# A planner's release latencies, its settings and 32-row pieces of a down-projection in a fused attention and MLP kernel

## The chip, the cores and the metric

The kernel runs on one core of one Trainium2 chip. A core has five engines with a queue each: TensorE (PE in the profile; its weight loads are shown as PEld), VectorE (DVE), ScalarE (ACT), GpSimd (POOL) and SyncE (SP, which here only issues DMAs). The metric is the device time of one execution in microseconds, the median of several runs. The kernel before takes 757.61 us (three runs, 757.32 to 758.09).

## The reference

Two branches work on the same `x` of 2048 tokens by 512 values, and a sigmoid gate per token mixes them:

```python
q, k, v = split(x @ wqkv)                 # 32 heads of 16 values
a = softmax(q @ k.T / 4) @ v @ wo         # attention over 2048 keys
h  = gelu(layernorm(x) @ w1)
x1 = x + shift_tokens(h) @ w2             # 4 groups of channels shifted by 1, -1, 2, -2 tokens
b  = x1 + gelu(layernorm(x1) @ w3) @ w4   # 512 -> 1792 -> 512
out = g * a + (1 - g) * b                 # g = sigmoid(sum(x * gate_w))
```

With 32 heads and 2048 x 2048 scores per head, the exponentials are the largest job: 134 million of them.

## The kernel before

**Attention tiles.** The queries are cut into 4 chunks of 512. A score tile is 128 keys by 512 queries of one head, and there are 32 x 16 x 4 = 2048 of them (`TOT`, line 933). They are grouped in 32 rounds: chunk, group of 8 heads, and one of two halves of the group, so that a round has 4 heads, each in a row tile of TensorE of its own, with 16 key tiles per head (line 1219). A score matmul (`qk_op`, line 1254) contracts over 32 rows, so up to four of them run at once in the four row tiles. The product with V (`take_pv`, lines 1465 to 1489) contracts over 128 keys and fills 17 of 32 columns, so four of those run at once in four column tiles; they add up in one bank of PSUM, the accumulator of the round.

**Two ways to an exponential.** Either ACT takes two or three score tiles, 1024 or 1536 columns, in one instruction straight from PSUM (`issue_act`, line 1352); how many is decided by `CAP2` and `CAP3`, the number of banks that ACT's tiles may hold together. Or DVE turns a tile into the bits of an approximation (line 1383), and for each two such tiles three shifted copies are made, by DVE (line 1426) or by POOL (line 1428). An ACT tile needs one product with V, a DVE tile four. `GP2` and `GP3` set how the three copies are shared out: normally DVE makes the first two and POOL the third; for a share `GP2` of the pairs POOL makes two; for a share `1 - GP3` DVE makes all three (`close_pair`, line 1403).

**The other matmuls.** The projections and the MLP are cut into groups of 512 output columns (`gen`, line 911). A group is a list of units, one per block of 128 in the contraction, and each unit is four matmuls into four column tiles of the group's bank. The down-projection `w4` (`mlp2_down`, line 1166) has 14 units over the 1792 inner values, and, but for the last chunk, four more with `wo` over the packed attention output `oD`. DVE empties the bank of a group.

**End of a round.** The accumulator is copied out (line 1501); a chain of small DMAs (lines 1503 to 1516) brings the denominators to a reciprocal and spreads them over the partitions (`bcs`), POOL multiplies (line 1518), and four DMAs pack the result into `oD` (line 1522), from which the `wo` units read.

**What sets the order.** The order of all instructions is worked out when the program is built, by a small event-driven model of the engines (`Sim`, line 154). Each piece of work is a `Job` with a hold (how long its engine is taken) and a latency (how long after that its results and buffers count as there). PE's next visit is picked by `pe_pick` (line 1651): first score tiles for ACT, then tiles for DVE; when there is no room for those, up to `MAXU` passes of products with V and group units. `pe_run` (line 335) gives each its time: 216 ns for a pass of 512 columns, a switch between row tiles, column tiles and the full array (`SWITCH`, line 155), and a release 275 ns after the end (`PE_LAT`, line 157). Some forty settings (`BASE`, line 445) steer it, and `STEPS` (line 470) changes them at given places: step n takes effect at score tile 8n. On the chip only the order on each queue remains; semaphores make an instruction wait for its data and for its buffers.

Of the kernel before, what the change touches and what calls it, by code (L numbers as in the profile page):

```python
# [98 lines left out]
class Job:  # L99
    __slots__ = ("eng", "hold", "lat", "deps", "prio", "fn", "acq", "frees", "at", "done", "start", "seq", "ready", "name", "port", "watch", "deps_tiles", "size")  # L100

    def __init__(self, eng, hold, lat, deps, fn, prio=5, acq=(), frees=(), at=0, name="", port=False):
        self.port = port
        self.eng, self.hold, self.lat, self.deps, self.fn = eng, hold, lat, list(deps), fn
        self.prio, self.acq, self.frees, self.at = prio, list(acq), list(frees), at
        self.done = self.start = None
        self.seq = 0
        self.ready = None
        self.name = name
        self.watch = []  # L110
        self.size = 0


class Op:
    __slots__ = ("mode", "tile", "fn", "done", "start", "ns", "frees", "name", "watch", "dst")

    def __init__(self, mode, tl, fn, ns=216.0, frees=(), name=""):
# [7 lines left out]
class Gen:  # L125


    def __init__(self, units, deps, at, name, acq="bank", due=None):
# [6 lines left out]
        self.skew = False  # L135

    def left(self):
        return any(self.cp[j] < len(self.units) for j in range(4)) if self.skew else self.pos < len(self.units)

    def take(self, j):  # L140
        k = self.cp[j]
        if k == len(self.units):
            return None
        self.cp[j] = k + 1
        o = self.units[k][j]
        if min(self.cp) == k + 1:
# [5 lines left out]


class Sim:
    SWITCH = {"row": 122.0, "col": 96.0, "full": 96.0}
    ISSUE = 4.0
    PE_LAT = 275.0

    def __init__(self, slots):
# [23 lines left out]
        self.readers = {}  # L183

# [12 lines left out]
    def place(self, job):  # L197

        for d in job.deps:
            if d.done is None:  # L200
                d.watch.append(job)
                return
        self.jobs[job.eng].append(job)
# [84 lines left out]
    def try_engine(self, e):  # L288
# [22 lines left out]
        for b in j.acq:  # L311
            self.take(b)
        j.start = self.t
# [11 lines left out]
        self.push(self.t + j.hold, None)  # L325
        self.pending -= 1
# [8 lines left out]
    def pe_run(self, ops):  # L335
        cur = self.t
        for o in ops:
# [5 lines left out]
            else:  # L343
                s = max(self.arr[o.tile], cur + self.ISSUE)
            if o.tile is None:
# [7 lines left out]
            self.push(s + o.ns + self.PE_LAT, lambda o=o: self.finish_op(o))  # L353
# [39 lines left out]
def kernel(  # L393
# [73 lines left out]
        ROT=2, DUE_SH=-14, AT_SH=0, HOLE=7, MAXG=1, CAP2=6, CAP3=0, LIMD=3, RES=0, GATE=2, E_PRIO=2, AFIRST=0, AGE=12000, ACC2=0, LIMA=3, JOIN=0,  # L467
# [3 lines left out]
        0: dict(DVE_STOP=13, SL1=200, B_LOW=2, DVE_WAIT=1, PV_IDLE=0.5, PRESS=26, DUE_SH=0, AT_SH=34, CAP3=5, GATE=4,  # L471
            E_PRIO=0.25),
        1: dict(GP2=0.8),
        2: dict(GP2=0.655),
        3: dict(PV_FULL=0.97, LIMA=2),
        5: dict(DVE_STOP=8, SL1=60),
        6: dict(P1_PRIO=0.279),
        7: dict(GP3=0.8, B_LOW=1),
        8: dict(S_PRIO=0.178, GP3=0.967, B_LOW=2, AFIRST=1),
        9: dict(P1_PRIO=0.312, GP2=0.8, SL1=200, PV_FULL=0.916, PV_IDLE=0.731, ROT=0, HOLE=2, AFIRST=0, LIMA=3),  # L480
        10: dict(S_PRIO=0.38),
        13: dict(AT_SH=118),
        14: dict(ROT=2, AT_SH=96),
        16: dict(AHEAD2=9, PV_IDLE=0.5),
        19: dict(GP3=0.8, JOIN=1),
        20: dict(DVE_WAIT=2, AT_SH=0),
        21: dict(AFIRST=2),
        22: dict(URG=8),
        23: dict(GP3=0.9, DVE_STOP=6, DVE_ALONE=-81, DVE_WAIT=1, AHEAD2=13, PV_FULL=0.947, MAXU=3, ROT=1, AT_SH=34,
            HOLE=0, JOIN=0),  # L490
        24: dict(GP2=1),
        25: dict(DVE_STOP=13),
        26: dict(DVE_STOP=8, MAXU=5),
        29: dict(SL0=0),
        30: dict(SL0=45),
        31: dict(AHEAD=5),
        33: dict(DVE_STOP=6),
        34: dict(PRESS=18, MAXU=3),
        35: dict(P1_PRIO=0.414, GP3=1, URG=5, DVE_ALONE=138, AHEAD=9, PV_FULL=0.813, PV_IDLE=0.731, PRESS=26, E_PRIO=0.1,
            AGE=6000, JOIN=1),  # L500
        37: dict(ROT=3),
        39: dict(P1_PRIO=0.136, DVE_ALONE=500, DVE_WAIT=4),
        40: dict(MAXU=7, HOLE=2),
        41: dict(URG=11, AT_SH=96),
        42: dict(DVE_STOP=8, IDLE_NS=374, DVE_WAIT=2),
        44: dict(P1_PRIO=0.312),
        45: dict(P1_PRIO=0.136),
        46: dict(AT_SH=69),
        47: dict(S_PRIO=0.178, AGE=3000, LIMA=2),
        48: dict(ROT=1),  # L510
        51: dict(URG=2),
        52: dict(DVE_WAIT=1),
        53: dict(AGE=20000),
        54: dict(PV_FULL=0.97),
        55: dict(DVE_ALONE=2, PV_FULL=0.916),
        56: dict(AT_SH=118),
        59: dict(MAXU=4, ROT=0),
        61: dict(DVE_ALONE=138),
        62: dict(AGE=1000000000),
        63: dict(AGE=20000),  # L520
        65: dict(URG=11, ACC2=1),
        69: dict(AHEAD2=16, MAXG=2, AGE=1000000000),
        70: dict(AHEAD2=13, MAXG=1, AGE=20000),
        71: dict(PV_FULL=0.813, ACC2=0, LIMA=4),
        72: dict(S_PRIO=0.214, ROT=3),
        73: dict(S_PRIO=0.178, AHEAD2=16, PV_FULL=0.916, ROT=0, MAXG=2, AGE=1000000000, ACC2=1, LIMA=2),
        74: dict(AFIRST=1),
        76: dict(PV_IDLE=0.117, AGE=20000),
        77: dict(HOLE=7),
        79: dict(ROT=1),  # L530
        80: dict(ROT=2),
        81: dict(B_LOW=1, MAXU=3),
        82: dict(GP3=0.633, ROT=0, MAXG=1),
        83: dict(GP2=0.5),
        84: dict(GP3=0.8, LIMA=4),
        85: dict(P1_PRIO=0.279, URG=5, DVE_ALONE=2, SL1=0, IDLE_NS=864, B_LOW=8, DVE_WAIT=2, PV_FULL=0.813, PRESS=57,
            MAXU=2, ROT=2, DUE_SH=-9, HOLE=0, CAP2=4, CAP3=0, GATE=3, E_PRIO=2, AFIRST=0, LIMA=2, JOIN=0),
        86: dict(PV_FULL=0.916, ROT=1),
        87: dict(HOLE=7, ACC2=0),
        88: dict(GP3=0.9, PV_FULL=0.86, E_PRIO=0.1),  # L540
        89: dict(PRESS=26, AGE=1000000000),
        90: dict(B_LOW=2),
        91: dict(GP2=1, GP3=0.8, EARLY=64, B_LOW=8, PV_FULL=0.916, PRESS=57, E_PRIO=2, AGE=20000),
        92: dict(GP2=0.5, EARLY=99),
        93: dict(URG=8, DVE_ALONE=-81, AHEAD=24, PV_FULL=0.813, CAP2=5, AGE=1000000000, ACC2=1),
        95: dict(DVE_ALONE=2, LIMD=4, E_PRIO=0.4),
        96: dict(DVE_ALONE=-81, LIMD=3, E_PRIO=2),
        97: dict(S_PRIO=0.214, GP2=0, GP3=0.967, URG=5, DVE_ALONE=2, B_LOW=5, DVE_WAIT=4, AHEAD=9, PV_IDLE=0.731,
            PRESS=18, ROT=2, HOLE=3, CAP2=4, E_PRIO=0.4, ACC2=0, LIMA=3),
# [1346 lines left out]
```

## Time and profile before

| | |
|---|---|
| median of the runs | 757.61 us |
| profiled execution: time, span | 757.9 us, 756.0 us |
| busy PE, ACT, DVE, POOL | 740.8, 738.0, 674.2, 423.0 us |
| exponentials on ACT: 1024 columns, 1536 columns | 560, 133 instructions |
| score tiles on DVE (line 1383) | 529 |
| copies on DVE, on POOL | 436, 359 |
| score matmuls, products with V | 2048, 3635 |

The share of busy time must be read with care. An instruction's span in the trace reaches from its start to the end of its write, and the next one on the same engine starts before that, so an engine is shown busy even where it could have done more. The rate of an engine is read from the distance between starts, or from a merged row of many like instructions. For TensorE the chain of work (in which every visit to row tiles and every visit to column tiles is one piece, with the time until the next) says more than the busy time.

### The profile page before, as it was taken

The numbers are of one execution on the slowest core, as the hardware profiler recorded it, in microseconds if no ns is written. First come the engines' busy times: TensorE is split into PE (matmuls) and PEld (weight loads), VectorE is DVE, ScalarE is ACT, GpSimd is POOL, SyncE is SP. The second block draws the span as 40 slices with busy tenths as digits, with TensorE's granted clock in tenths as the row PEclk, the third lists the DMA queues.
The fourth block names the chain that finished last, engine by engine and source line by source line (L and its number), as shares of the span: only waits on it lengthen the run. The fifth ranks groups of instructions, "written<-read, shape, count | busy, mean of one in ns | idle before, by whom it ended". The sixth has DMA issues, their size and how long they took to land.

```text
span 756.0 us, 23489 instructions
## 1 busy us (share of the span) xinstructions
PE 740.8 (98%) x9464; PEld 213.2 (28%) x9464; DVE 674.2 (89%) x1399; ACT 738.0 (98%) x714; POOL 423.0 (56%) x421
## 2 busy tenths in 40 slices
PE   8999999999999999999999899999999999999997
PEld 4334222222222222223222222222222322222222
DVE  5899988889999999999999796798888989999886
ACT  6999999999999999999999899999999999999995
POOL 2265467776665465554554653477776855553431
PEclk9999999999999999999999999999999999999999
DMA  9423331012412200132001100100200000000001
GB/s 201 139 72 75 71 65 26 21 45 66 114 34 73 79 17 21 27 100 79 10 24 35 30 25 27 35 6 20 49 17 20 21 13 26 25 28 21 20 20 33
DMA packets 67093, 34.59 MB, mean 46 GB/s; under 512 B 46748, under 2 KB 62380, under 8 KB 66984
## 3 DMA queue, kind: packets, MB, share of 16 engines
q1 hardware_dynamic: 66040, 32.56, 17.0%
q8 instruction: 74, 1.21, 0.7%
q10 hardware_dynamic: 944, 0.52, 0.2%
q14 instruction: 35, 0.29, 0.1%
HBM read 17.40 MB, written 6.81 MB: 32 GB/s over the span
## 4 chain that ended last, share of the span: by engine, by line
PE 81%; ACT 11%; DVE 4%; issue 2%; DMA 0%; POOL 0%; ACTq 0%; DVEq 0%; POOLq 0%
PE banks L1257 28%; PE banks L1481 28%; PE banks L918 23%; ACT prob L1352 10%; DVE prob L1383 1%; DVE prob L1426 1%; ACT hB L1162 1%; PE banks L897 0%; PE banks L1817 0%; DMA oD<-oT 0%; ACT hT L1162 0%; DVE st L1065 0%; ACT L1352 0%; DVE V L1006 0%; DVE xn L1085 0%
## 5 line engine op out<-in xcount | busy, mean ns | idle before, releaser
L1352 ACT ACTIVATE prob<-banks 128x1024 bf16<-128x1024 f32 (+1 forms) x693 | 693.5, 1281 | 3.2 <-PE banks L1257 3.0
L1428 POOL TENSOR_SCALAR prob<-prob 128x1024 uint16<-128x1024 uint16 x359 | 370.0, 1045 | 272.5 <-DVE prob L1426 129.3
L1383 DVE TENSOR_SCALAR prob<-banks 128x512 uint16<-128x512 f32 x529 | 351.6, 682 | 45.1 <-PE banks L1257 41.8
L1481 PE MATMUL banks<-prob,V 128*17 128x512 bf16 (+1 forms) x3635 | 315.1, 381 | 0.4 <-POOL prob L1428 0.2
L1257 PE MATMUL banks<-q,kT 32*128 32x512 bf16 x2048 | 279.1, 384 | 6.2 <-ACT prob L1352 3.3
L1426 DVE TENSOR_SCALAR prob<-prob 128x1024 uint16<-128x1024 uint16 (+1 forms) x436 | 174.3, 437 | 6.5 <-PE banks L1481 3.0
L1257 PEld LDWEIGHTS <-kT 32*128 32x128 bf16 x2048 | 70.3, 91 | 316.0 <-ACT prob L1352 288.1
L1481 PEld LDWEIGHTS <-V 128*17 128x17 bf16 (+1 forms) x3635 | 70.3, 88 | 119.0 <-issue 97.9
L918 PE MATMUL banks<-xnT,w 128*32 128x512 bf16 x1152 | 93.2, 383 | 0.1
L1518 POOL TENSOR_TENSOR oT<-accsb,bcs 128x512 bf16<-128x512 f32 x31 | 39.5, 1274 | 43.4 <-DVE prob L1426 27.1
L918 PE MATMUL banks<-w,hT 128*32 128x512 bf16 x704 | 63.3, 383 | 0.0
L918 PEld LDWEIGHTS <-w 128*32 128x32 bf16 x1920 | 41.2, 95 | 44.9 <-issue 27.2
L918 PE MATMUL banks<-w,hB 128*32 128x512 bf16 x448 | 40.0, 382 | 0.1
L918 PE MATMUL banks<-w,w 128*32 128x256 bf16 (+1 forms) x768 | 40.0, 310 | 0.0
L918 PE MATMUL banks<-wo,oD 128*32 128x512 bf16 x224 | 29.1, 383 | 2.3 <-DMA oD<-oT 2.3
L1155 DVE CAST hB<-banks 128x512 bf16<-128x512 f32 x28 | 19.1, 683 | 4.0 <-PE banks L918 3.9
L1501 DVE COPY accsb<-banks 128x512 f32<-128x512 f32 x31 | 21.2, 682 | 1.6 <-PE banks L1481 1.6
L918 PEld LDWEIGHTS <-hT 128*32 128x32 bf16 x704 | 16.3, 95 | 19.1 <-issue 12.2
L1065 DVE BATCH_NORM_STATS2 st<-x_sb 128x6 f32<-128x512 bf16 x32 | 21.7, 679 | 0.0
L918 PE MATMUL banks<-w,wq 128*32 128x512 bf16 x256 | 20.0, 382 | 0.7 <-ACT w L949 0.7
L1155 DVE CAST hT<-banks 128x512 bf16<-128x512 f32 x28 | 19.1, 681 | 0.5 <-PE banks L918 0.4
L918 PEld LDWEIGHTS <-hB 128*32 128x32 bf16 x448 | 10.7, 95 | 12.3 <-issue 8.3
(90 smaller groups left out, 240.3 us busy)
## 6 DMA issues: line engine op xcount, KB each, us to landing
bcs<-rr SPq DMA_DIRECT2D x124, 64.0 KB
xn_dram<-xn SPq DMA_DIRECT2D x32, 128.0 KB
w<-in_B_w_dram SPq DMA_DIRECT2D x5, 512.0 KB
oD<-oT SPq DMA_DIRECT2D x124, 16.0 KB
w<-in_B_w_dram SPq DMA_DIRECT2D x4, 448.0 KB
out_dram<-ot SPq DMA_DIRECT2D x14, 128.0 KB
x_sb<-in_A_x_dram SPq DMA_DIRECT2D x3, 512.0 KB
w<-in_A_wqkv_dram SPq DMA_DIRECT2D x2, 256.0 KB
```

The lines of the kernel that those rows point to most:

```text
L918: units.append([Op("col", j, lambda j=j, lf=lf, rf=rf, n0=n0, n1=n1, st=st, sp=sp: nc.tensor.matmul(get()[32 * j:32 * j + 32, n0:n1], lhsT ...
L1065: a = dve(600, deps, lambda: nc.vector.bn_stats(out=sb.slot[:], in_=x_sb[:, t, :]), prio=6, at=at, acq=[sb])
L1155: pre.append(evac(g, PSUM_NS, lambda ps, m=m: nc.vector.tensor_copy(out=h2()[:, m, :], in_=ps[:])))
L1162: ge = act(93 + 427 * FT + (0 if n else 3050), pre, lambda h2=h2: nc.scalar.activation(out=h2(), in_=h2(), func=ACT.Gelu_apprx_tanh), prio=-1)
L1257: o = Op("row", i, lambda: nc.tensor.matmul(dst(), lhsT=kT[G][32 * i:32 * i + 32, kt * P:(kt + 1) * P], rhs=qbuf[G, c].slot[32 * i:32 * i ...
L1352: job = act(hold, ops, lambda: nc.scalar.activation(out=prob[:, pb.cut(), :].bitcast(BF16), in_=unit()[:, rb.cut(), :], func=ACT.Exp, scal ...
L1383: return nc.vector.tensor_scalar(out=prob[:, b0.cut() if w == 2 else b0.bufs[h0].slot, :], in0=unit()[:, rb.cut() if w == 2 else rb.bufs[0 ...
L1426: return nc.vector.tensor_scalar(out=cut(k), in0=cut(0), scalar1=float(SHIFT * k), scalar2=None, op0=ALU.add)
L1428: return nc.gpsimd.tensor_scalar(out=cut(k), in0=cut(0 if both else 2), scalar1=1.0, scalar2=float(SHIFT * (k if both else 1)), op0=ALU.mu ...
L1481: return nc.tensor.matmul(one(accs[r])[32 * i:32 * i + n, :], lhsT=lhs(n), rhs=rhs(), start=st and not edge, stop=True, tile_position=(0, ...
L1501: e = dve(PSUM_NS, round_ops[r], lambda: nc.vector.tensor_copy(out=ab.slot[:], in_=one(accs[r])), acq=[ab], prio=0, frees=[accs[r], Call(a ...
L1518: n = gp(1250, d3, lambda: nc.gpsimd.tensor_tensor(out=ob.slot[:], in0=ab.slot[:], in1=bb.slot[:], op=ALU.mult), acq=[ob], frees=[ab, bb], ...
```

## The change

Five things are done together.

1. **Latencies of the model.** The release after a matmul falls from 275 ns to 215 ns (score tile for ACT), 250 ns (for DVE) or 255 ns (all others). ACT's latency rises from 160 to 180, DVE's falls from 210 to 165, POOL's from 200 to 110. A bank that ACT or DVE has read counts as free 100 or 75 ns after the hold instead of after the whole latency, and a matmul into it is timed no earlier than 195 or 168 ns after the hold (`EARLY`, `USABLE`). The switch to row tiles goes from 122 to 104 ns, that to column tiles from 96 to 104. An exponential's fixed part goes from 55 to 51.5 ns. The packing DMAs of line 1522 are given 3700 ns until they land instead of 2200.
2. **Spread transfers.** The second to fourth DMA of each set of four (the transposes of line 1095 and 1579, the spread of line 1515, the packing of line 1522) used to be planned behind the landing of the first; they are now planned as soon as the first has taken the buffer (`need`). The packing of a round's second half no longer is planned behind that of its first half (`pack0` goes).
3. **Row pieces.** Where a visit to row tiles leaves a row tile free, a 32-row piece of a unit of `w4` may go there: a quarter of the contraction, all 128 output columns, added to the group's bank. The last units of the group are taken for it, from the end, four pieces replacing four column-tile matmuls. At most three units are open, at most one piece goes into a visit, a piece in another row tile than the last one waits until the last one's end is known to have been seen, and at least `ROWM` units must lie between; `ROWM` is 99 (off) in parts of `STEPS`, and 3, 5 or 7 elsewhere.
4. **Settings.** `STEPS` is replaced as a whole. Among the rest: `CAP3`, up to now 5 or 6 in steps 0 to 84, 147 to 162 and from 249 on, stays at 0 until step 253; `GP2` is 0.8 or 1 in most of steps 4 to 121 and 175 to 241, low in 122 to 174 (before: high in steps 1 to 91, 139 to 146 and 160 to 205, low in 97 to 138 and 207 to 248).
5. **Release of the inner buffer.** The buffer of the 1792 inner values is freed by the last matmul of a `w4` group, not by that of its 14th unit.

```diff
+    def unit_of(self, j):
+        k = self.cp[j]
+        return k if k < self.top else len(self.units) - 1 if k == self.top and not self.rows else None
...
+    def row_piece(self, free, know, least):
+        if self.last and self.last.n > know:
+            free = [x and i == self.last.tile for i, x in enumerate(free)]
+        if not any(free):
+            return None
+        for e in self.rows:
+            for i in range(4):
+                if e[1] >> i & 1 and free[i]:
+                    e[1] &= ~(1 << i)
+                    if not e[1]:
+                        self.rows.remove(e)
+                    return self.piece(e[0], i)
+        if len(self.rows) < 3 and min(self.cp) >= 1 and self.top - 1 - max(self.cp) >= least:
+            self.top -= 1
+            i = free.index(True)
+            self.rows.append([self.top, 15 & ~(1 << i)])
+            return self.piece(self.top, i)
+        return None
...
-    SWITCH = {"row": 122.0, "col": 96.0, "full": 96.0}
+    SWITCH = {"row": 104.0, "col": 104.0, "full": 96.0}
...
-    PE_LAT = 275.0
+    EARLY = {"ACT": 100.0, "DVE": 75.0}
+    USABLE = {"ACT": 195.0, "DVE": 168.0}
...
+            if j.need is not None and j.need.slot is None:
+                continue
...
+        soon = [b for b in j.frees if isinstance(b, Call) or b.cls == "bank"] if e in self.EARLY else []
...
-        return sim.add(Job("DVE", hold, 210.0, deps, fn, **kw))
+        return sim.add(Job("DVE", hold, 165.0, deps, fn, **kw))
...
-        return sim.add(Job("POOL", hold, 200.0, deps, fn, port=True, **kw))
+        return sim.add(Job("POOL", hold, 110.0, deps, fn, port=True, **kw))
...
+        def by_rows(k, i):
+            lf, rf = mms[k][:2]
+            rows = slice(32 * i, 32 * i + 32)
+            o = Op("row", i, lambda: nc.tensor.matmul(get(), lhsT=lf(0, P)[rows], rhs=rf()[rows], start=False, stop=True,
+                                                      tile_position=(32 * i, 0), skip_group_check=True), name=name)
+            o.dst = [g.buf]
+            return o
...
-            if k:
-                js[k].deps.append(js[0])
+            js[k].need = tb if k else None
...
-            g.units[FT - 1][-1].frees.append(bb)
+            g.ops[-1].frees.append(bb)
...
-            d4.append(dma(2200.0, [n] + d4[:1], lambda j=j: nc.sync.dma_start(
+            d4.append(dma(3700.0, [n] + ([j_clr] if r == NR - 2 else []), lambda j=j: nc.sync.dma_start(
...
         if ops:
+            per = [sum(o.tile == i for o in ops) for i in range(4)]
+            least = K.ROWM if sim.tiles < TOT - 128 else 99
+            know = max(sim.pe_know, sim.bank_know[ops[0].dst[0].slot])
+            for g in active:
+                if g.by_rows:
+                    x = g.row_piece([x < max(per) for x in per], know, least)
+                    if x:
+                        per[x.tile] += 1
+                        ops.insert(1, x)
             sim.pe_run(ops)
```

More of the change, by code (lines that the diff above doesn't have):

```diff
@@ L1615, in gen_new, with at_work @@
         return best
+    def at_work():
+        return next((g for g in active if g.can()), None)
     def gen_ready():
[L1618 removed]
+        return at_work() or gen_new()
     def begin(g):
@@ L1635, in gen_op @@
                     return o
-        if more and len(active) < K.MAXG and (not active or active[-1].skew):
+        if more and sum(g.can() for g in active) < K.MAXG and (not active or active[-1].skew):
             g = gen_new()
```

510 lines of the change are left out of this document (266 added, 244 removed).

## The prediction

> **What bounds the kernel now.** I read the page first, then the waits, the chain of work by stages, and ACT's and DVE's own rows.
>
> ```profile
> span 756.0 us, 23489 instructions
> PE 740.8 (98%) x9464; PEld 213.2 (28%) x9464; DVE 674.2 (89%) x1399; ACT 738.0 (98%) x714; POOL 423.0 (56%) x421
> PE 81%; ACT 11%; DVE 4%; issue 2%; DMA 0%; POOL 0%; ACTq 0%; DVEq 0%; POOLq 0%
> L1383 DVE TENSOR_SCALAR prob<-banks 128x512 uint16<-128x512 f32 x529 | 351.6, 682 | 45.1 <-PE banks L1257 41.8
> L1481 PE MATMUL banks<-prob,V 128*17 128x512 bf16 (+1 forms) x3635 | 315.1, 381 | 0.4 <-POOL prob L1428 0.2
> L1426 DVE TENSOR_SCALAR prob<-prob 128x1024 uint16<-128x1024 uint16 (+1 forms) x436 | 174.3, 437 | 6.5 <-PE banks L1481 3.0
> ```
>
> ACT and PE are both shown at 98%, which settles nothing, since spans overlap. ACT's real rate comes from a merged row of pairs and from the two forms:
>
> ```profile
> 363.91 53.44 ACT L1352 ACTIVATE prob<-banks 128x1024 bf16<-128x1024 f32 x58
> L1352 ACT ACTIVATE prob<-banks 128x1024 bf16<-128x1024 f32 x560 | 552.5, 1198 | 3.0 <-PE banks L1257 3.0
> L1352 ACT ACTIVATE prob<-banks 128x1536 bf16<-128x1536 f32 x133 | 216.8, 1630 | 0.2 <-ACT prob L1352 0.2
> ```
>
> 58 pairs in 53.44 us, less one span of 1.20, over 57 steps: 0.917 us per pair, 0.459 per tile. A triple spans 0.432 longer, so 1.349. Hence 560 x 0.917 + 133 x 1.349 = 693 us of the 737 between the first exponential and the last visit of the rounds is ACT's score work alone (the rest is mostly gelu and table loads). ACT is full: the time falls only if it gets fewer tiles or loses fewer gaps.
>
> The waits and the chain tell how near PE is:
>
> ```profile
> PEld L1257 <- ACT prob L1352: 288.1, 630, 1.5
> ...
> POOL prob L1428 <- DVE prob L1426: 129.3, 92, 9.4
> ```
> ```profile
> 97.22 0.32 PE banks L1257 x2
> 97.54 0.55 PE banks L918 x8
> ...
> 105.11 0.39 PE banks L1257 x3
> 105.50 0.76 PE banks L918 x12
> 106.26 0.32 PE banks L1257 x3
> ```
> ```profile
> 298.70 0.37 PE banks L1257 x2
> 299.07 0.54 PE banks L1481 x8
> 299.61 0.39 PE banks L1257 x4
> ```
>
> 630 times a visit to score tiles waits for ACT to free a bank, so nearly every one of the 693. A visit without wait takes 0.32, two passes in column tiles 0.55, three 0.76: 0.21 to 0.215 per pass, about 0.105 and 0.11 for the two switches. So each visit costs PE 0.43 beside its passes. In the pair stage (third fence) 0.37 + 0.54 = 0.91 is ACT's 0.917; PE needs 0.86 of it. In the dense stage (second fence) eight visits with about three passes each take 9.04 us, 1.13 each, of which PE needs 0.43 + 3 x 0.215 = 1.075: 95%.
>
> Over the whole run PE needs 693 x 0.43 = 298 for visits. Its passes:
>
> ```profile
> 0.00:756.00 756.00, 274.39 (x3552) 78.97 (x3552) 1.00 0.18 46
> ```
>
> Length, then PE and PEld, of line 918 alone; 512 of them (the V projection) are half as long, so (3635 + 3040 + 256) / 4 = 1733 passes x 0.215 = 373. Sum 671 of 737: 91%. PE is the second bound, 9% behind.
>
> DVE by stages (columns: stretch, length, then busy time of PE, PEld, DVE, ACT and POOL):
>
> ```profile
> 95.00:190.00 95.00, 92.68 (x1145) 26.59 (x1142) 83.56 (x160) 94.24 (x79) 67.63 (x67) 1.00 0.18 45
> ...
> 285.00:330.00 45.00, 44.79 (x485) 10.15 (x485) 44.33 (x97) 45.00 (x50) 24.18 (x24) 1.00 0.14 32
> ...
> 410.00:500.00 90.00, 87.03 (x1111) 23.60 (x1103) 70.81 (x142) 87.21 (x88) 46.36 (x44) 1.00 0.09 26
> 500.00:600.00 100.00, 99.64 (x1290) 28.34 (x1287) 88.57 (x170) 99.97 (x104) 75.94 (x74) 1.00 0.09 21
> ...
> 700.00:747.00 47.00, 46.87 (x574) 12.46 (x571) 39.69 (x79) 46.97 (x48) 19.76 (x19) 1.00 0.07 18
> ```
>
> In the second row DVE is full; in the other four it is idle for 11.4, 19.2, 11.4 and 7.3 us, 49.3 in sum, while ACT is full. That is the room: tiles that DVE could take from ACT.
>
> **The change part by part.** The base is the profiled execution, 757.9 us (0.3 above the median of the runs).
>
> *Packing given 3700 ns.* The present plan lets PE start `wo` units on `oD` too early, and PE, which works in order, stands still with score tiles behind it:
>
> ```profile
> 415.78 1.71 DMA oD<-oT
> 418.53 1.77 DMA oD<-oT
> ```
> ```profile
> 413.54 0.51 SPq L1522 DMA_DIRECT2D oD<-oT  x1
> ...
> 415.78 3.33 SPq L1522 DMA_DIRECT2D oD<-oT  x3
> ```
> ```profile
> 418.51 1.02 ACT L1352 ACTIVATE prob<-banks 128x1024 bf16<-128x1024 f32 x1 [1.16 <-PE banks L1257]
> 421.16 172.13 ACT L1352 ACTIVATE prob<-banks 128x1024 bf16<-128x1024 f32 x180 [1.63 <-PE banks L1257]
> ```
>
> ACT loses 1.16 + 1.63 = 2.8 us. With the later landing in the model, and DMAs two to four issued behind the first instead of 2.2 us later, both gaps should go: -2.8 (bounds 0 and -3.5, the two waits).
>
> *Spread transfers.* SP issues the same DMAs, closer together. SP already stands 121.8 us behind POOL's product (row below), so three issues of about 0.5 us in a row may delay another round's DMA by 1.5 us; who waits for it is POOL, idle for 44% of the span. Cost 0. If that cover went, one such delay would reach PE once per chunk, at most 4 x 1.5 = 6; in the other direction `bcs` and `oT` come free 2 us sooner, worth 0 while no engine of the chain waits for them.
>
> ```profile
> SPq L1522 <- POOL oT L1518: 121.8, 25, 8.2
> ```
>
> *Triples go.* `CAP3` = 0 turns 399 tiles from 133 triples into 199.5 pairs: 199.5 x 0.917 - 133 x 1.349 = +3.5 us on ACT (bounds 0, should free banks pay it back, and +3.5).
>
> *DVE's share.* A DVE tile costs DVE a conversion and its part of the copies:
>
> ```profile
> 299.02 1.78 DVE L1426 TENSOR_SCALAR prob<-prob 128x1024 uint16<-128x1024 uint16 x5
> 300.72 1.88 DVE L1383 TENSOR_SCALAR prob<-banks 128x512 uint16<-128x512 f32 x3
> ```
>
> (1.88 - 0.68) / 2 = 0.60, and (1.78 - 0.44) / 4 = 0.34 for a copy of a pair, of which DVE makes 436 / 264.5 = 1.65: 0.60 + 0.28 = 0.88. Banks that count as free up to 135 ns sooner and releases 20 to 90 ns sooner let the plan place a tile where it now leaves DVE idle. I take half of the 49.3 us: 24.7 / 0.88 = 28 tiles, -28 x 0.459 = -12.9 us on ACT. Bounds: none (0) and all (56 tiles, -25.7). I take the middle since the stage at 285 to 330 shows that a full DVE is possible, though in a stage with little beside attention. More copies for POOL in steps 97 to 121 and 206 to 231, fewer in 139 to 146 and 160 to 174, are part of this half: some 25 copies, 8.5 us of DVE, 10 tiles.
>
> The Trainium skill, SBUF — State Buffer, section "SBUF: two separate sides", says that VectorE in its two-port modes and GpSimd hold a shared port pair exclusively, the loser waiting for the whole instruction. By it the copies moved to POOL would free nothing, and the sum would be 4.6 us higher; the 129.3 us that POOL waits behind DVE's copies agree with it as far as they go.
>
> *Row pieces.* A `w4` group has 18 units. With 7 units kept between, some five or six visits find the distance and give one piece each: 6 x 16 groups, about 100 pieces, 25 units, -5.4 us of PE. Their cover is the visit's free row tile (2048 score matmuls over 693 visits, 2.96 each, so one is free). On ACT nothing. If that cover is missing, each piece lengthens its visit by 0.215. Bounds for PE: +21.5 and -12 (twice as many pieces and a bit).
>
> *Inner buffer freed four units later.* 4 x 0.215, under 1 us, hidden by the slack in the due times; 0.
>
> **Sum.** 757.9 - 2.8 + 3.5 - 12.9 = 745.7: 746 us.
>
> What is late next is PE. With 557 tiles on DVE there are 745.5 pairs, and if each has its visit, 745.5 x 0.43 = 320.6; passes 1733 + 28 x 3 / 4 - 25 = 1729, 371.7; together 692, in 745.7 - 20.9 = 724.8 between the same two ends: 95.5%. The forecast thus needs of PE over the whole run what the dense stretch shows, 95%. Two pairs in one visit (four tiles) would each give back 0.43.
>
> **The rivals.**
>
> B, the larger gain: DVE takes nearly all 56 tiles: 757.9 - 2.8 + 3.5 - 25.7 = 733. For it: idle DVE beside a full ACT in four stages. Against: PE would stand at 97%, above any stretch quoted.
>
> C, slower, by PE: 52 visits more at 0.43 are 22 us, and 692 us of PE work fit into the old time only from 692 / 737 = 93.9% on. Today's mean is 91%. At 93%: 692 / 0.93 + 20.9 = 765. For it: the triples stand where PE's passes are thickest. Against: the dense stretch.
>
> D, nothing gained in order: -2.8 and +3.5 cancel, 758.6. For it: ACT is full now, and shorter latencies in a model shorten nothing on the chip. Against: the idle DVE.
>
> E, the pieces don't share a visit: 100 x 0.215 unhidden instead of hidden, (692 + 5.4 + 21.5) / 0.955 + 20.9 = 774. Against: the quoted visit with four tiles takes 0.39, that with two 0.37. The Trainium skill, TensorEngine Tiling (Array Packing), "Gotcha 1: PSUM Pressure", says that different row tiles cannot access the same bank at once; the change keeps two such pieces apart by `know`, and no row here shows one.
>
> **How the numbers follow.** Forecast 0.56 (741 to 751 by a quarter more or less than the 28 tiles, and the bounds above), B 0.17, C 0.15, D 0.06, E 0.04; 0.02 is left for others. A measurement can tell about 0.2% of this kernel from no change, 1.5 us. Faster: 0.56 + 0.17, and 0.01 of the rest, 0.74. Same: D, 0.06. Slower: C, E and 0.01, 0.20. The range is 733 (B's end) to 765 (C's).
>
> **What would show it.** DVE conversions near 557 instead of 529, exponentials all pairs and near 745; no DMA `oD` pieces in the chain near the start of the second half; DVE idle halved in the four stages. Visits in the dense stage must show passes of 0.215 with no wait longer than now. Row pieces appear as matmuls of `w` and `hT` or `hB` with 32 rows; right if visits that hold one stay near 0.32. Wrong if ACT's idle time before line 1352 grows by more than some us, released by PE (C), or if the conversions stay at 529 (D).

## The result and the profile after

The changed kernel takes 755.4 us (median of 20 runs, 753.07 to 757.7) beside 758.1 for the kernel before (20 runs): a ratio of 0.9966, with a 95% interval of 0.9956 to 0.9976. It is faster by 0.34%, some 2.6 us. Forecast were 746 us, a gain of 1.5%. The direction was right and nearly four fifths of the gain did not come.

These are rows of the page of the changed kernel: span, busy time, the shares of the chain that ended last, and four groups. Lines moved with the edit: exponentials on ACT are now line 1408, conversions on DVE 1439, copies on DVE and POOL 1482 and 1484, score matmuls 1313, products with V 1537, column-tile passes of the groups 964, row pieces 975.

```profile
span 753.0 us, 23698 instructions
...
PE 738.9 (98%) x9520; PEld 213.2 (28%) x9520; DVE 685.8 (91%) x1422; ACT 732.4 (97%) x768; POOL 458.2 (61%) x456
...
PE 85%; DVE 5%; ACT 4%; DMA 4%; issue 1%; POOL 0%; SPq 0%; DVEq 0%; POOLq 0%; ACTq 0%
...
L1439 DVE TENSOR_SCALAR prob<-banks 128x512 uint16<-128x512 f32 x551 | 364.0, 683 | 29.6 <-PE banks L1313 25.6
...
L1482 DVE TENSOR_SCALAR prob<-prob 128x1024 uint16<-128x1024 uint16 (+1 forms) x437 | 172.6, 440 | 5.8 <-PE banks L1537 1.7
...
L1484 POOL TENSOR_SCALAR prob<-prob 128x1024 uint16<-128x1024 uint16 x394 | 405.7, 1048 | 255.4 <-DVE prob L1482 108.7
```

DVE now converts 553 tiles (two of the 551 instructions take two), 24 more than the 529 of before. The copies of these tiles all went to POOL: 394 instead of 359 there, 437 instead of 436 on DVE. In the chain ACT falls from 11% to 4%, and a DMA appears with 4% where there was none.

The stages whose idle DVE the forecast counted, in the same columns as there (the last one is 44 us long instead of 47):

```profile
95.00:190.00 95.00, 94.17 (x1168) 25.55 (x1165) 87.28 (x174) 94.94 (x98) 66.52 (x65) 1.00 0.23 63
285.00:330.00 45.00, 44.97 (x528) 10.93 (x518) 42.71 (x89) 45.00 (x50) 30.67 (x30) 1.00 0.09 25
410.00:500.00 90.00, 89.47 (x1130) 23.38 (x1130) 85.55 (x182) 89.95 (x99) 48.69 (x46) 1.00 0.10 30
500.00:600.00 100.00, 99.79 (x1268) 26.20 (x1265) 92.14 (x181) 100.00 (x110) 65.88 (x65) 1.00 0.10 26
700.00:744.00 44.00, 43.56 (x509) 11.80 (x506) 41.39 (x89) 43.88 (x47) 21.18 (x20) 1.00 0.07 18
```

DVE is idle there for 7.7, 4.5, 7.9 and 2.6 us (first, third, fourth and fifth row): 22.6 instead of 49.3. That is the half that was forecast. ACT stays full in all of them.

So the planned part came, and the time is lost elsewhere. ACT's own rows show the place. A row merges instructions that follow each other; the bracket is the idle time ahead of it.

```profile
186.25 151.50 ACT L1408 ACTIVATE prob<-banks 128x1024 bf16<-128x1024 f32 x165
338.06 8.36 ACT L1408 ACTIVATE prob<-banks 128x1024 bf16<-128x1024 f32 x9 [0.31 <-PE banks L1313]
349.79 2.18 ACT L1408 ACTIVATE prob<-banks 128x1024 bf16<-128x1024 f32 x2 [3.37 <-PE banks L1313]
...
369.44 13.29 ACT L1408 ACTIVATE prob<-banks 128x1024 bf16<-128x1024 f32 x14 [0.67 <-POOL prob L1484]
383.02 235.97 ACT L1408 ACTIVATE prob<-banks 128x1024 bf16<-128x1024 f32 x257 [0.28 <-PE banks L1313]
```

From 383 us on nothing stops ACT for 236 us: the two stops near 418 and 421 are gone. In their place stands a stop of 3.37 us at 349.8, with smaller ones around it. PE's rows and SP's at that time:

```profile
344.80 0.39 PE L1313 MATMUL banks<-q,kT 32*128 32x512 bf16 x3
347.67 0.40 PE L964 MATMUL banks<-xnT,w 128*32 128x512 bf16 x4 [2.48 <-DMA xnT<-xn_dram]
348.94 0.40 PE L964 MATMUL banks<-xnT,w 128*32 128x512 bf16 x4 [0.88 <-DMA xnT<-xn_dram]
349.28 0.39 PE L1313 MATMUL banks<-q,kT 32*128 32x512 bf16 x3
```

```profile
345.04 2.43 SPq L1152 DMA_TRANSPOSE xnT<-xn_dram  x2
347.57 1.91 SPq L1572 DMA_DIRECT2D bcs<-rr  x4
350.04 1.12 SPq L1152 DMA_TRANSPOSE xnT<-xn_dram  x1
```

PE stands behind a unit of the up-projection `w3` that reads `xnT`, and waits first for one transposing DMA, then for a second. Both were issued only at 345.0 and 346.2. The score tiles for ACT are queued behind that unit, so ACT stops too.

The stop has an aftermath. The column before the last two in the next rows is the share of its clock that TensorE was granted. After PE's two waits it falls to a half for 3.4 us; in the run described first below, which has no such stop, it stays at 1 there (second fence). The last fence shows pieces of the chain of work at half and again at full clock: eight column-tile matmuls take 0.96 us instead of 0.55.

```profile
345.00:350.00 5.00, 1.65 (x22) 0.51 (x19) 1.03 (x2) 1.63 (x3) 2.77 (x3) 1.00 0.43 94
350.00:353.40 3.40, 3.40 (x28) 0.57 (x24) 3.04 (x5) 3.24 (x4) 1.05 (x1) 0.50 0.41 103
```

```profile
350.00:353.40 3.40, 3.40 (x53) 1.20 (x57) 3.37 (x7) 3.39 (x2) 2.28 (x3) 1.00 0.46 104
```

```profile
350.86 0.96 PE banks L1537 x8
...
353.70 0.55 PE banks L964 x8
```

How long this lasts differs from run to run. The mean granted clock of the 20 runs lies between 0.992 and 0.999; the ten runs with 0.997 or more have a median of 754.9 us, the ten with 0.995 or less one of 756.9.

The two transposing DMAs that PE waits for carry chunk 3, while the waiting unit belongs to chunk 1. The plan shows how that came about. All four column tiles of a group unit read the buffer, and `take` hands the release of the buffer to the column tile that comes last in the count; when another column tile's last matmul ended before that, its releases were already given, and they are given again by the last one. For the `xnT` buffer of chunk 1 the planner recorded 15 releases for 14 groups: one group gave two, at 325.4 and 330.9 us of the plan's clock, and the buffer counted as free at 337.4, while the 14th group was to be read at 339.6 to 340.7. So the first two transposes of chunk 3 were ordered ahead of that group. On the chip order decides: the group waits for the two transposes, and its first two blocks of the contraction are read from chunk 3. By the old rule of planning the second would have stood behind the landing of the first, at 342.6 on the plan's clock, and so behind the group.

The rule of counting is the same in the kernel before, and releases the same buffer early there too: its trace shows all four transposes of chunk 3 issued between 317.6 and 324.2 us, and the last two groups of chunk 1 reading the buffer after them, from 329.3 and from 345.8 us on. They landed before PE came to these groups, so nothing waited. New in the changed kernel is not the wrong order but that the transposes stand directly ahead of their reader. In both kernels these groups so take values of chunk 3 where those of chunk 1 belong, in all four blocks in the kernel before and in two in the changed one.

### The profile page after: what moved, and what is told of

Same layout as the page of the kernel before. It is cut to its first block, busy times and chain, and to the rows that moved or that the text cites. A ratio compares the mean times of both kernels' runs of the same rounds, so it can differ in the third digit from the quotient of the medians.

```text
span 753.0 us, 23698 instructions
## 1 busy us (share of the span) xinstructions
PE 738.9 (98%) x9520; PEld 213.2 (28%) x9520; DVE 685.8 (91%) x1422; ACT 732.4 (97%) x768; POOL 458.2 (61%) x456
## 4 chain that ended last, share of the span: by engine, by line
PE 85%; DVE 5%; ACT 4%; DMA 4%; issue 1%; POOL 0%; SPq 0%; DVEq 0%; POOLq 0%; ACTq 0%
PE banks L1537 30%; PE banks L1313 29%; PE banks L964 24%; ACT prob L1408 3%; DMA pk<-den 2%; DVE prob L1439 2%; DVE prob L1482 1%; DMA den<-accsb 1%; ACT hT L1218 1%; PE banks L943 0%; DVE st L1122 0%; PE banks L1890 0%; DMA zE_dram<-ot 0%; POOL prob L1484 0%; DMA xnT<-xn_dram 0%
## 5 line engine op out<-in xcount | busy, mean ns | idle before, releaser
L1484 POOL TENSOR_SCALAR prob<-prob 128x1024 uint16<-128x1024 uint16 x394 | 405.7, 1048 | 255.4 <-DVE prob L1482 108.7
L1439 DVE TENSOR_SCALAR prob<-banks 128x512 uint16<-128x512 f32 x551 | 364.0, 683 | 29.6 <-PE banks L1313 25.6
L1537 PE MATMUL banks<-prob,V 128*17 128x512 bf16 (+1 forms) x3707 | 318.3, 382 | 1.3 <-POOL prob L1484 0.6
L1313 PE MATMUL banks<-q,kT 32*128 32x512 bf16 x2048 | 283.2, 385 | 2.8 <-ACT prob L1408 0.9
L964 PE MATMUL banks<-xnT,w 128*32 128x512 bf16 x1152 | 91.1, 384 | 3.4 <-DMA xnT<-xn_dram 3.4
L975 PE MATMUL banks<-wo,oD 32*128 32x512 bf16 x72 | 27.7, 384 | 0.0
L964 PE MATMUL banks<-wo,oD 128*32 128x512 bf16 x152 | 20.1, 384 | 0.1
```

Source lines behind the costliest of these rows:

```text
L964: units.append([Op("col", j, lambda j=j, lf=lf, rf=rf, n0=n0, n1=n1, st=st, sp=sp: nc.tensor.matmul(get()[32 * j:32 * j + 32, n0:n1], lhsT ...
L975: o = Op("row", i, lambda: nc.tensor.matmul(get(), lhsT=lf(0, P)[rows], rhs=rf()[rows], start=False, stop=True, tile_position=(32 * i, 0), ...
L1313: o = Op("row", i, lambda: nc.tensor.matmul(dst(), lhsT=kT[G][32 * i:32 * i + 32, kt * P:(kt + 1) * P], rhs=qbuf[G, c].slot[32 * i:32 * i ...
L1439: return nc.vector.tensor_scalar(out=prob[:, b0.cut() if w == 2 else b0.bufs[h0].slot, :], in0=unit()[:, rb.cut() if w == 2 else rb.bufs[0 ...
L1484: return nc.gpsimd.tensor_scalar(out=cut(k), in0=cut(0 if both else 2), scalar1=1.0, scalar2=float(SHIFT * (k if both else 1)), op0=ALU.mu ...
L1537: return nc.tensor.matmul(one(accs[r])[32 * i:32 * i + n, :], lhsT=lhs(n), rhs=rhs(), start=st and not edge, stop=True, tile_position=(0, ...
```

## The experiments

What had to be told apart: is the stop at 349.8 the main loss (the theory), or is PE's amount of work, or the model's shorter latencies? Parts of the change can't be undone one by one, because the whole order is then planned anew. So in the first eight runs the plan is kept, and only what the instructions do, or where in a queue they stand, is edited.

**The two transposes behind their last reader.** The plan is that of the changed kernel; on SP's queue the first two transposes of chunk 3 stand behind the last group that reads the buffer.

```diff
             js[k].need = tb if k else None
+            if which and c == NCH - 1 and k < 2:
+                js[k].emit_at = 342600.0 + k
...
-        self.emit(self.t, ...)
+        self.emit(max(self.t, j.emit_at), ...)
```

> The changed kernel with the same plan; only the first two transposes of chunk 3 into the xnT buffer now stand behind the last w3 group that reads that buffer, instead of ahead of it. Theory (ACT is full, so a stop of PE that starves ACT is never given back): the 3.4 us gap of ACT at 349.8 us goes and with it some of the smaller gaps up to 383 us, 3.4 to 5 us off the changed kernel, about 0.991 of the kernel before. Rival (PE is the bound and catches up in any case, or the transposes then stop somebody else): less than 1 us, 0.996 or more.

Measured: 749.85 us (749.1 to 750.78), ratio to the kernel before 0.9885 (0.9866 to 0.9905). That is 5.5 us less than the changed kernel, and more than the 3.4 to 5 expected, for two DMAs that stand elsewhere on one queue. All four runs had a granted clock of 1.000. ACT's rows of this run:

```profile
119.04 58.79 ACT L1411 ACTIVATE prob<-banks 128x1024 bf16<-128x1024 f32 x64 [1.49 <-PE banks L1316]
...
195.14 154.41 ACT L1411 ACTIVATE prob<-banks 128x1024 bf16<-128x1024 f32 x168 [0.21 <-PE banks L1316]
...
364.42 250.87 ACT L1411 ACTIVATE prob<-banks 128x1024 bf16<-128x1024 f32 x273
```

From 195.14 ACT runs through to its gelu at 349.5, and from 364.42 for 251 us more, so the smaller stops after the large one had come of it as well. Both profiles have the same ACT instructions in the same order, so their starts can be compared one by one. The changed kernel is 1.2 us ahead of this run at 342.6 us and 3.7 behind it at 383.0, and stays 3.7 behind to the end: the stretch with the stop costs 4.9 us, and nothing later does. The stop of 3.37 and half of the 3.4 us at half clock make 5.1. The theory holds, but the cost is that of the stop and of the lower clock after it. A gap of 1.49 us at 119.0 is new in this profile, though the plan up to there is that of the changed kernel, which shows none, so it is not the edit's; it is taken up below. This version is faster than both kernels.

**The pieces as column passes.** Same plan; the 84 row pieces are left out of the visits, and their 21 units run as ordinary column passes ahead of the group's last unit.

```diff
         o = self.units[k][j]
+        if k == len(self.units) - 1 and self.top < k:
+            gone = [self.units[m][j].fn for m in range(self.top, k)]
+            o.fn = lambda fn=o.fn: [f() for f in gone + [fn]][-1]
...
-            self.emit(s, self.writes(o))
+            self.emit(s, None if o.piece else self.writes(o))
```

> The changed kernel with the same plan, but the 21 units of w4 that go as 84 row pieces are done as column passes just before the group's last unit: 21 passes more for PE, 4.5 us of its work. Theory (ACT is the bound, PE has some slack): 0 to 1.5 us slower than the changed kernel, 0.9966 to 0.9985 of the kernel before. Rival (PE is the bound): 4 to 5 us slower, 1.002 or more. If pieces cost something in their visits: faster than the changed kernel.

Measured: 760.83 us (760.31 to 763.58), ratio 1.0033 (1.0022 to 1.0044): 5.4 us slower than the changed kernel. 21 passes of 0.215 us are 4.5 us of PE, and the run pays all of it, as the rival said. (Six runs of each with the same granted clock, 0.995, have medians of 760.5 and 756.3 us, 4.2 apart.) ACT's rows show where; each stop is released by score matmuls that came too late:

```profile
387.59 23.43 ACT L1412 ACTIVATE prob<-banks 128x1024 bf16<-128x1024 f32 x25 [0.46 <-PE banks L1317]
411.30 16.61 ACT L1412 ACTIVATE prob<-banks 128x1024 bf16<-128x1024 f32 x18 [0.27 <-PE banks L1317]
428.90 17.58 ACT L1412 ACTIVATE prob<-banks 128x1024 bf16<-128x1024 f32 x19 [1.00 <-PE banks L1317]
```

In the same stretch the changed kernel has a single row. In this order PE has no room left there, so the pieces are worth what they take off it.

**Packing DMAs one behind the other, in the kernel before.** The second to fourth packing DMA of each round are put directly behind the first on SP; the wait of PE on `oD` should go if their spacing was the cause.

```diff
+            d4[j].lead = (d4[0], 1.0 * j) if j else None
...
-        self.emit(self.t, ...)
+        self.emit(j.lead[0].start + j.lead[1] if j.lead else self.t, ...)
```

> The kernel before with its plan; only the second to fourth packing DMA of each round are issued directly behind the first. Theory (PE's two stops at 415.8 and 418.5 us come from the late issue of these three): the two gaps of ACT go, 2.8 us, 0.9963. Rival (the packing lands late whatever its place): unchanged, 1.000.

Measured: 761.72 us (758.18 to 764.58), ratio 1.0041 (1.0026 to 1.0055), slower by 3.5 us, which neither theory had. PE and SP of this run, at the place of the two stops, and PE's clock behind it (columns as above):

```profile
419.77 0.38 PE L919 MATMUL banks<-wo,oD 128*32 128x512 bf16 x1 [3.21 <-DMA oD<-oT]
```

```profile
415.99 2.41 SPq L1523 DMA_DIRECT2D oD<-oT  x4
```

```profile
420.50:423.90 3.40, 3.40 (x28) 0.63 (x26) 1.27 (x5) 2.05 (x2) 1.05 (x1) 0.50 0.00 0
```

The two stops became one. PE stands for 3.2 us at once, instead of 0.9 and 1.3, and then again has half its clock for 3.4 us; ACT loses 4.0 us there instead of 2.8. By ACT's starts some 1.6 us of the profiled run's loss of 3.0 fall at this place and 1.2 before 98 us. Over the twelve runs the time goes with the granted clock: 758.18 us at 0.999, 764.58 at 0.991.

The four issues take 2.4 us, the last lands near 419.6, 3.6 us after the first issue: that is the 3700 ns which the change writes into the model. But the product that they pack had itself come 2.4 us later, at 414.7, because on SP the spread DMAs ahead of it now stand behind the packing of the round before. So this run does not test the spacing with all else equal. It shows that packing one behind the other does not remove the stops by itself; that the later place of the `wo` units does it in the changed kernel is argued, not shown.

**Less work for ACT.** On top of the run with the late transposes, the exponentials of ACT are taken over 448 of each 512 columns.

```diff
+    nc.gpsimd.memset(prob[:, :, 448:512], 0)
...
-        job = act(hold, ops, lambda: nc.scalar.activation(out=prob[:, pb.cut(), :].bitcast(BF16), in_=unit()[:, rb.cut(), :],
+        job = act(hold, ops, lambda: nc.scalar.activation(out=prob[:, pb.cut(), 0:448].bitcast(BF16), in_=unit()[:, rb.cut(), 0:448],
```

> As the first kernel of this set, but ACT's exponentials take 448 of 512 columns of each tile (one eighth of ACT's part of the exponentials is left out; those probabilities are zero). A pair costs ACT 107 ns less, 80 us in all. Theory of the prediction (PE needs 692 us and is just behind ACT): 715 to 730 us, PE now waiting for nothing. If PE were the bound already: above 740. If PE were far from it: below 690.

Measured: 735.96 us (735.11 to 737.03), ratio 0.9702 (0.9683 to 0.9722), 13.9 us less than the run that it builds on. ACT's group (columns as on the page):

```profile
L1412 ACT ACTIVATE prob<-banks 128x896 bf16<-128x896 f32 x746 | 646.4, 916 | 26.0 <-PE banks L1317 14.1 <-PE banks L1541 2.1 <-POOL prob L1488 0.5
```

An eighth of 746 x 0.917 = 684 us is some 85 us less for ACT, and only 14 arrive, fewer than expected. The chain of work of this run lies to 82% on PE, 11% on DVE and 1% on ACT, so in this order PE is the next bound, about 2% below ACT.

**Less work for PE.** On the same base, the products with V take 448 of 512 queries, except a round's first.

```diff
-            return nc.tensor.matmul(one(accs[r])[32 * i:32 * i + n, :], lhsT=lhs(n), rhs=rhs(), ...
+            m = 512 if st or edge else 448
+            return nc.tensor.matmul(one(accs[r])[32 * i:32 * i + n, 0:m], lhsT=lhs(n), rhs=rhs()[:, 0:m], ...
```

> As the kernel with the two transposes moved (e1, 749.85 us), but each product with V after a round's first in its column tile takes 448 of 512 queries (an eighth of most products is left out). Some 890 passes are 27 ns shorter, 24 us less work for PE, all else the same. Theory (ACT is the bound, PE close behind and stopping it only in places): ACT's work of about 738 us stays, 3 to 9 us faster, 741 to 747. Rival (PE is the bound): 15 us or more, 735 or less.

Measured: 750.31 us (749.21 to 750.96), ratio 0.9884 (0.986 to 0.9909): no gain over 749.85. Its busy row:

```profile
PE 726.8 (97%) x9520; PEld 214.9 (29%) x9520; DVE 686.6 (92%) x1422; ACT 731.4 (98%) x768; POOL 458.1 (61%) x456
```

The kernel here leaves out an eighth of most products. 3 to 9 us had been expected; PE, with some 24 us less to do, gives nothing, so the amount of PE's work is not what is left over. Together with the run with less work for ACT and the one with column passes: ACT first, PE directly behind.

**DVE's reciprocal later.** In the run with late transposes DVE waits 4.5 us in sum for the small DMA ahead of the reciprocal, up to 2.3 us at once, and the gap at 119.0 stands behind such a wait. Here the reciprocal, the product after it and the DMA behind them stand 1.2 us of the plan later on their queues.

```diff
-        self.emit(self.t, ...)
+        self.emit(max(self.t, j.emit_at) + j.shift, ...)
...
+        r1.shift = r2.shift = d2.shift = 1200.0
```

> As e1, but in the order of DVE the two small operations on the denominators (reciprocal and product with the gate) and the DMA behind them stand 1.2 us later, so that DVE does a conversion or two first and does not stand before a DMA that has not landed. Theory (late DMAs that hold DVE, and PE behind it, make the small gaps): DVE's wait for that DMA falls from 4.5 us to under 1.5, 1 to 3 us faster than e1, 0.985 to 0.988 of the kernel before. Rival (the chain of the round is now 1.2 us longer and something else waits for it): no faster than e1, 0.9885 or more.

Measured: 756.75 us (755.28 to 757.63), ratio 0.9977 (0.9966 to 0.9988), 6.9 us slower than its base. The waits of DVE and POOL (sum, times, longest):

```profile
POOL oT L1580 <- DMA bcs<-rr: 15.5, 12, 2.2
...
DVE pk L1568 <- DMA pk<-den: 1.2, 1, 1.2
```

DVE's wait fell from 4.5 to 1.2, and POOL's wait for the spread DMAs rose from 6.5 to 15.5. The wait only moved. DVE's groups show what it cost; first the base, then this run:

```profile
L1485 DVE TENSOR_SCALAR prob<-prob 128x1024 uint16<-128x1024 uint16 x434 | 172.5, 443 | 6.2 <-PE banks L1540 2.2 <-POOL prob L1487 1.0 <-ACT prob L1411 0.7
```

```profile
L1485 DVE TENSOR_SCALAR prob<-prob 128x1024 uint16<-128x1024 uint16 x434 | 180.8, 462 | 6.7 <-PE banks L1540 3.9 <-ACT prob L1411 0.4 <-POOL prob L1487 0.3
```

The same 434 copies take 8.3 us more. In the base 22 of the 437 copies last longer than 600 ns, here 41, and each of these ends 0.28 us after the end of an operation of POOL. One of the places, in DVE's rows and POOL's:

```profile
337.32 1.76 DVE L1485 TENSOR_SCALAR prob<-prob 128x1024 uint16<-128x1024 uint16 x3
```

```profile
336.85 1.27 POOL L1580 TENSOR_TENSOR oT<-accsb,bcs 128x512 bf16<-128x512 f32 x1 [1.41 <-DMA bcs<-rr]
```

POOL's product started late, at 336.85, and ran until 338.12; the DVE copy that started at 337.32 took 1.09 us instead of some 0.42 and ended 0.3 after it.

**POOL's product later.** The product and the packing stand 1.2 us later, the reciprocal where it was.

```diff
+        n.shift = 1200.0
...
+            d4[j].shift = 1200.0
```

> As e1, but in the order of POOL its product at a round's end, and the four packing DMAs behind it, stand 1.2 us later, so that POOL makes a copy first where the spread has not landed. Theory (waits for late DMAs on engines that work in order make the gaps that are left): POOL's wait for the spread falls from 6.5 us to under 2, 0.5 to 2 us faster than e1, 0.986 to 0.988. Rival (the time is set by ACT's own work by now, or the copies that POOL would make first are not ready either): within 0.7 us of e1.

Measured: 751.76 us (750.59 to 753.53), ratio 0.9911 (0.9895 to 0.9928): 1.9 us slower than the base (this run and the next were on another chip, where the kernel before took 758.5 us instead of 758.2), though POOL's wait for the spread fell from 6.5 to 1.5 us. Neither theory had that.

```profile
PE banks L976 <- DMA oD<-oT: 1.2, 1, 1.2
```

Packing now lands after its first reader, a row piece, and PE waits for it once.

**Both later.** Reciprocal 1.2 us, product and packing 1.8 us.

> As e6 (DVE's two operations 1.2 us later, 7 us slower than e1), and POOL's product and the packing DMAs 1.8 us later. Theory (e6 lost its time because the spread then landed 1.2 us later and POOL stood before it, 15.5 us instead of 6.5): POOL's wait falls under 4 us and the loss goes, 0.985 to 0.990. Rival (DVE's new order is worse in itself): no better than e6, 0.9965 or more.

Measured: 764.06 us (763.54 to 768.2), ratio 1.0082 (1.0059 to 1.0105), 7.3 us slower than with the reciprocal alone. The theory that these waits make the loss falls.

```profile
L1485 DVE TENSOR_SCALAR prob<-prob 128x1024 uint16<-128x1024 uint16 x434 | 186.4, 475 | 7.0 <-PE banks L1540 3.4 <-POOL prob L1487 0.6 <-issue 0.6
```

```profile
POOL oT L1580 <- DVE prob L1485: 25.4, 12, 3.5
```

DVE's copies grow by another 5.6 us, and POOL's product now waits 25.4 us behind them. In the base it waits 8.4. The waits of DVE and POOL for DMAs went, and collisions of POOL with DVE came for them: 44 copies now last longer than 600 ns.

**The release given once, and planned anew.** `take` keeps the releases of a unit until its last column tile.

```diff
         if min(self.cp) == self.cp[j]:
-            for x in self.units[k]: ...
+            o.frees += self.kept.pop(k, [])
+        else:
+            self.kept.setdefault(k, []).extend(o.frees)
+            o.frees = []
```

> The changed kernel with the planner's early release repaired: a group's buffers are freed once, by the last of its four column tiles. The plan is made anew, so the order differs from about 100 us on, under settings chosen for the other plan. Theory (the settings fit one plan only): no stop of PE for the transposes, but slower than the changed kernel all the same, 760 to 775 us. Rival (the gain lies in the model and its settings in general): 748 to 752, as e1.

Measured: 764.82 us (764.13 to 765.14), ratio 1.008 (1.0056 to 1.0103). With the fault mended but the settings kept, the order as a whole is another one, DVE gets 544 tiles, and a place with a long run of column passes turns up:

```profile
444.50 0.61 PE L965 MATMUL banks<-wo,oD 128*32 128x512 bf16 x8
444.93 3.20 PE L965 MATMUL banks<-w,hT 128*32 128x512 bf16 x56
447.96 1.04 PE L965 MATMUL banks<-wo,oD 128*32 128x512 bf16 x16
448.82 1.69 PE L1538 MATMUL banks<-prob,V 128*17 128x512 bf16 x28
```

```profile
449.30 21.25 ACT L1409 ACTIVATE prob<-banks 128x1024 bf16<-128x1024 f32 x23 [5.40 <-PE banks L1538]
```

For six us no visit to score tiles was planned, and ACT stood for 5.4.

**One nanosecond in the kernel before.** `PE_LAT` 276 instead of 275, nothing else.

> The kernel before, the planner's release after a matmul given as 276 ns instead of 275; nothing else. Theory (settings fit one plan only): a different order, 10 to 30 us slower than the kernel before. Rival (a good model matters, not the one plan): within 3 us of it.

Measured: 779.16 us (778.79 to 779.52), ratio 1.027 (1.0238 to 1.0301). One nanosecond in the model costs 21 us. That the settings were found for one order, and the order is now another, is the theory that forecast this, and no run here speaks against it.

## Why the prediction was right in direction and too large

*Packing, -2.8: right.* Both stops are gone. The run with the packing in a row shows that spacing the DMAs closer does not do this alone; that the later place of the `wo` units does is argued.

*Triples, +3.5: right.* One triple and 746 pairs are left, so 132 triples went: 132 x (1.5 x 0.917 - 1.349) = +3.5.

*DVE's share, -12.9: the mechanism right, the size a little off.* 24 tiles instead of 28, so 24 x 0.459 = -11.0; idle DVE was halved. In the forecast a tile cost DVE 0.88 us with its copies. In the run DVE's conversions grew by 12.4 us (351.6 to 364.0) and its copies fell by 1.7, because the copies went to POOL. By the rule that was weighed there (the Trainium skill, SBUF — State Buffer, "SBUF: two separate sides": the shared port pair is held for a whole instruction) they would have freed nothing. The traces agree with the rule: all 17 copies longer than 600 ns in the kernel before, and all 21 in the changed one, end 0.28 us after the end of an operation of POOL. But with 35 copies more on POOL the cost to DVE hardly grew, from some 8 us in sum to some 9 (mean copy 437 and 440 ns), because the kernel keeps most copies of the two engines apart: it lets POOL's instructions wait for DVE's by dependencies of its own (`in_port_order`). For that reason POOL's wait of 129.3 us behind DVE's copies, which the forecast took as agreeing with the rule, does not show it.

*Row pieces, 0 on ACT, -5.4 on PE: right.* 84 pieces, 21 units, 4.5 us. The forecast looked for pieces of `w` with `hT` or `hB`; as the units are taken from the end, 72 of the 84 are pieces of `wo` with `oD`, and 12 of `w` with `hT`. As forecast, a visit with a piece takes hardly longer. Pieces of the chain of work, each with the time until the next:

```profile
387.26 0.54 PE banks L1537 x8
387.80 0.35 PE banks L1313
388.15 0.00 PE banks L975
388.15 0.01 PE banks L1313 x2
388.16 0.55 PE banks L964 x8
388.70 0.37 PE banks L1313 x3
```

The visit with a piece takes 0.36, the next one, without, 0.37. Over all visits of three matmuls the medians are 321 ns with a piece and 321 without, of four 325 and 325; one matmul more costs a visit 3 to 4 ns. So E, in which the pieces don't share a visit, is shown wrong, and the run with column passes shows the gain: 5.4 us, or 4.2 at equal clock.

*PE as the next bound: right, though it had less to do than forecast.* Visits did not grow to 745: PE's rows show 708 visits for the 746 pairs and DVE's tiles, so many of them serve two. With 0.43 for each and some 1730 passes of 0.215, an estimate from the forecast's own prices, PE needs 676 us, 93% of the time with late transposes instead of 95.5%. That is one reason why C did not happen. But the run with 4.5 us more of PE work pays for all of it, as C has it, so C was near.

*Spread transfers, "Cost 0": the step that failed.* "SP issues the same DMAs, closer together ... who waits for it is POOL." The set of four transposes into `xnT` is in this part of the change, and its reader is PE. The forecast followed `bcs` and `oD` and gave the transposes no term. In the new order two of them stand directly ahead of the last reader of the buffer that they overwrite. The cost, by the run that moves them alone, is 5.5 us: PE's stop and the half clock after it. The forecast's bound of 6 us, for the case that the cover goes, holds this number by luck, for it was worked out for another delay, of SP's queue. That the early start of the second one is due to the new `need` is argued from the plan, not shown; the early release, which lets the first one go, is in both kernels.

The terms with their measured sizes: 757.9 - 2.8 + 3.5 - 11.0 = 747.6. With the transposes late, 749.85 was measured, so 2.3 us are left, and the 5.5 us of the stop are the rest of what the changed kernel lacks. ACT's starts show where the 2.3 lie: the time beyond 0.904 us for each pair and 1.33 for each triple (the medians from start to start) sums to 12.1 us in the kernel before, of which 2.8 are the two packing stops, and to 12.8 in the run with late transposes. So many small gaps grew from 9.3 to 12.8, by 3.5 in the profiled run, which at 750.78 us is 3.2 above the sum. What makes them is open. It is not the amount of PE's work, for with 24 us less of that they sum to 12.9; and the three runs that moved the small waits one by one gained nothing.

## What to carry to other kernels

Time that a planner saves arrives only as far as the in-order queues let it: here its own clock promised 10.7 us (the last product with V through at 730.7 instead of 741.5), and one badly placed pair of DMAs took back about half of it. Before a forecast gives a moved DMA the cost 0, ask of each buffer that it writes who reads it last, on which queue that reader stands, and what is queued behind it. And where settings were searched for one order, test a part with the order held fixed, because another edit, as that of one nanosecond here, measures a new order and not the part. And when PE has stood still, look at its granted clock behind the stop: here that made the loss larger than the stop.

## What the runs showed of the hardware

- A 32-row matmul in a free row tile of a visit costs the visit 3 to 4 ns: visits of two, three and four matmuls have medians of 318, 321 and 325 ns, those of three and four whether or not one of them is a piece. By its own span a piece takes 384 ns.
- After PE stood still, TensorE's granted clock fell to a half: for 3.4 us after waits of 2.5 and 0.9 us (the changed kernel), of 3.2 (packing in a row) and of 1.9 (one nanosecond), for 10.2 us in the profile of the run with column passes. After waits of 0.9 and 1.3 us in the profile of the kernel before, and of one of 2.0 with both later, it did not. From which wait on it falls, no run here shows.
- A copy from SBUF to SBUF on DVE that meets an operation of POOL ends 0.28 us after it: all of those over 600 ns, 17 in the kernel before, 21 in the changed one, 41 and 44 in the runs with the reciprocal and with both later. The usual copy takes 0.42 us. Conversions from PSUM don't show that: 681 ns in the base and in the run with the reciprocal later, where the copies went from 443 to 462.
- Four small packing DMAs issued one behind the other take 3.6 us from the first issue to the last landing, 2.4 of them for the issues on SP.
